# Fused attention and two MoE layers: three of six float32 attention tiles moved to float16 parts with DMA transpositions, and a new list of the front

## The chip, the cores and the metric

The kernel runs on one core of one Trainium2 chip. The metric is the device time of one execution in microseconds; smaller is better. The core has a matmul engine (TensorE, PE in the profile, with its weight loads as PEld), a vector engine (VectorE, DVE), a scalar engine (ScalarE, ACT), GpSimd (POOL) and SyncE (SP), whose queue issues most DMAs.

## The reference

The block-sparse attention (local band of 32 keys and 24 block summaries) feeds a dense layer with a clipped gate, and its output feeds a mixture of experts in which each token goes to one of eight experts.

```python
# attention: q, k, v are (2, 8, 768, 64)
k_sum = k.reshape(B, H, nb, block, D).max(axis=3)      # block = 32
v_sum = v.reshape(B, H, nb, block, D).mean(axis=3)
scores_l = scale * q @ k.T      # kept where |i - j| < 16
scores_s = scale * q @ k_sum.T + log(block)
a = softmax(concat(scores_l_masked, scores_s))
attn = a @ concat(v, v_sum)
...
# dense layer, x = attn as (1536, 512)
h = x @ w_in                                           # (1536, 2048)
g = h * np.clip(h + 3.0, 0.0, 6.0) / 6.0
x2 = g @ w_out                                         # (1536, 512)
...
# experts: one of 8 for each token, by argmax of x2 @ w_gate
h = np.maximum(xe @ w1[e], 0.0)                        # F = 1024
out[mask] = gate_w[mask, None] * (h @ w2[e])
```

## The kernel before

The 1536 tokens are 12 tiles u of 128, six to a batch. Attention goes tile by tile and in two groups g of four heads: scores (`s`), masking and row maximum (`t`, `nm`), exponentials with their row sums (`e`). Then the probabilities must be turned, because the product with V contracts over keys, and there are two forms of this, chosen for each tile by `F32_T`.

In the float32 form (tiles 0 to 5 before) VectorE takes the reciprocal of the row sums (`r`, `rc`), POOL spreads it over a diagonal matrix (`dg`, line 464), and TensorE multiplies the probabilities by the diagonal, which turns and normalises them in one go (`px`, lines 476 and 479, 16 matmuls of a group). ScalarE and VectorE copy the result out of PSUM (`pc`, `pd`, lines 488 and 490), and TensorE multiplies by V in float32 (`pv`, line 500, 16 matmuls of a group). The result comes out already transposed, and is split into a high and a low float16 part by ScalarE (`xa`) and VectorE (`xp`, line 556). The summaries of V for this form lie in `v2f`, which shares its memory with `v2`.

In the float16 form (tiles 6 to 11 before) ScalarE makes the high part of the probabilities (`pa`, line 453), POOL the low part (`pp`, lines 458 and 459), and a DMA on SP's queue transposes both (`px`, line 470). V is split into parts as well (`va`, `vd`). The product is 40 float16 matmuls of a tile (`pv`, line 517); then VectorE normalises (`n`, line 542), ScalarE and POOL split (`xa`, `xp`, lines 551 and 560), and a second DMA transposes x (`xx`, line 577).

The dense layer takes two tiles at a time (index j): `la` is one of eight groups of 24 matmuls of its first product (line 589), `lr`, `lm`, `lg`, `lp` are the gate on ScalarE, VectorE, ScalarE and POOL, `lb` the second product (line 626). Its weights come as 64-bit floats in 32 chunks of 512 KB (`wl`, 16 of w_in and then 16 of w_out) and are turned into float32 by three integer passes on VectorE (`wx`, `wy`, `ww`), scaled and rounded on ScalarE (`wa`, `wb`) and given a low part by POOL (`wp`). `la` with number m needs chunks 2m and 2m+1.

The order of the early work is written out by hand in the string `FRONT`: each name is a step, and each engine executes the instructions of its steps in this order. Loads of K and q (`kl`, `ld`), copies of V rows (`vu`) and transpositions stand in the same list and go to SP's queue in its order. The string `THEN` holds steps with due positions that are sorted in between later steps. Behind the front come the remaining tiles of attention, the dense layer, the routing of tokens, and the experts, whose steps are chosen by branches on the counts of tokens.

Of the kernel before, what the change touches and what calls it, by code (L numbers as in the profile page):

```python
# [83 lines left out]
FRONT = """
    km0.0 km0.1 km0.2 km0.3 km0.4 km0.5 kf0 s0.0 s0.1 t0.0 s1.0 t0.1 kl1.0 vm0.0 nm0.0 nm0.1 e0.0 t1.0 vm0.1 wl3
    nm1.0 e0.1 r0.0 vm0.2 rc0.0 dg0.0 wx0 e1.0 px0.0 r0.1 wy0 rc0.1 vm0.3 ww0 wl4 pc0.0 dg0.1 pd0.0 wa0 r1.0
    vm0.4 wb0 rc1.0 wp0 px0.1 wx1 dg1.0 vm0.5 pc0.1 ld2 pd0.1 wl5 wy1 vm0.6 wl6 km1.0 px1.0 pvs0 ww1 wx2 wa1
    pd1.0 wb1 wy2 wp1 pvd0 pv0.0 wg pvc0 ww2 pc1.0 pv0.1 wx3 wa2 wx4 s1.1 xa0 wy3 wb2 s2.0 kl1.1 t1.1 wp2 xp0
    nm1.1 wy4 e1.1 t2.0 s2.1 wx5 vu1 r1.1 nm2.0 vu2 rc1.1 e2.0 ww3 dg1.1 kl1.2 wx6 wa3 px1.1 ww4 wb3 r2.0 wl7
    wy5 wp3 pv1.0 ld3 pc1.1 pd1.1 wa4 rc2.0 t2.1 pv1.1 wb4 dg2.0 wy6 xa1 vu3 wp4 px2.0 xp1 nm2.1 la0.0 pc2.0  # L90
    pd2.0 e2.1 wx7 ww5 wy7 wl8 r2.1 pv2.0 ww6 lr0.0 rc2.1 wl9 lm0.0 s3.0 dg2.1 wa5 ww7 wa6 t3.0 lg0.0 wb5 lp0.0
    s3.1 km1.1 wb6 nm3.0 wl10 wp5 kl1.3 wx8 la0.1 wa7 e3.0 km1.2 wp6 wy8 ww8 wb7 r3.0 la0.2 wx9 lr0.1 wp7 rc3.0
    wl11 wy9 wa8 lm0.1 dg3.0 wb8 ww9 lg0.1 wp8 km1.3 la0.3 lr0.2 wl12 lm0.2 lp0.1 wa9 lg0.2 wb9 lp0.2 px2.1
    lr0.3 wp9 lm0.3 pc2.1 ld4 pd2.1 wx10 px3.0 lg0.3 t3.1 lp0.3 pv2.1 pc3.0 pd3.0 wy10 nm3.1 xa2 vu4 ww10 s4.0
    e3.1 xp2 pv3.0 t4.0 wl13 s4.1 r3.1 nm4.0 wa10 rc3.1 dg3.1 e4.0 kl1.4 px3.1 wx11 wb10 r4.0 wy11 wp10 pc3.1
    ld5 rc4.0 t4.1 dg4.0 ww11 wl14 pd3.1 wa11 px4.0 wx12 nm4.1 wb11 wy12 e4.1 wp11 km1.4 ww12 pv3.1 vml1.0 pd4.0
    vml1.2 pc4.0 r4.1 s5.0 vu5 rc4.1 xa3 wx13 dg4.1 la0.4 wl15 wx14 wa12 wy13 wb12 wy14 vha0 wp12 ww13 wl16 xp3
    lr0.4 pv4.0 ww14 wa13 lm0.4 wl17 px4.1 t5.0 wb13 lg0.4 wp13 vhd0 wa14 la0.5 ld6 pc4.1 lp0.4 wb14 wx15 vml1.1
    nm5.0 wp14 wy15 e5.0 s5.1 pd4.1 la0.6 ww15 kl1.5 t5.1 lr0.5 vha1 lm0.5 wl18 wx16 wa15 pv4.1 vhd1 lg0.5 wb15
    wy16 lp0.5 la1.0 lr0.6 r5.0 vha2 wp15 lm0.6 rc5.0 lg0.6 ww16 dg5.0 wl19 nm5.1 la1.1 lr1.0 lp0.6 wa16 wx17  # L100
    e5.1 lm1.0 wy17 la1.2 km1.5 lg1.0 ww17 wb16 lp1.0 kf1 lr1.1 wl20 wp16 wa17 lm1.1 s6.0 lr1.2 r5.1 wb17 la1.3
    lg1.1 wx18 wp17 rc5.1 wy18 lp1.1 lm1.2 wx19 lg1.2 lb0.0 dg5.1 ww18 lr1.3 wy19 wl21 lp1.2 wa18 lm1.3 wb18
    ww19 lg1.3 px5.0 vhd2 wp18 wl22 vml1.3 wa19 vml1.4 la0.7 t6.0 pc5.0 lp1.3 wb19 wx20 wp19 pd5.0 wy20 s6.1 xa4
    wx21 lr0.7 nm6.0 lb0.1 xp4 e6.0 wy21 lm0.7 ww20 lg0.7 ww21 pv5.0 wl23 lp0.7 wl24 wa20 la1.4 wa21 wb20 wb21
    wp20 pa6.0 wp21 la1.5 wx22 lr1.4 wy22 pp6.0 lm1.4 wx23 lg1.4 ww22 lb0.2 lp1.4 lr1.5 px6.0 wy23 wl25 lm1.5
    wa22 wx24 wb22 ww23 lg1.5 wp22 la1.6 wl26 wy24 wa23 lp1.5 ww24 wb23 wl27 wp23 wa24 px5.1 lr1.6 wb24 lm1.6
    lb0.3 wp24 pc5.1 ld7 pd5.1 t6.1 lg1.6 lp1.6 nm6.1 pv5.1 e6.1 la1.7 wx25 wy25 xa5 r6 pa6.1 ww25 rc6 wl28
    pp6.1 xp5 wa25 s7.0 lr1.7 la2.0 t7.0 wb25 wp25 lm1.7 wx26 lg1.7 nm7.0 wy26 lp1.7 lb0.4 e7.0 ww26 lr2.0 pa7.0
    lm2.0 vm1.0 la2.1 vha3 wx27 pp7.0 lg2.0 vhd3 wl29 wa26 lp2.0 wb26 wy27 vml1.5 la2.2 lr2.1 ww27 wp26 wl30
    lm2.1 wa27 wx28 lg2.1 wy28 wb27 la2.3 lp2.1 lr2.2 ww28 wl31 init lm2.2 wp27 wa28 wx29 lg2.2 wy29 lb0.5 wb28  # L110
    lp2.2 wx30 lr2.3 ww29 wp28 lm2.3 wa29 wy30 lg2.3 vm1.1 wb29 ww30 la2.4 lp2.3 vha4 wx31 wa30 wp29 vhd4 wb30
"""

THEN = """
    wp30 51.05, wy31 52.5, ww31 52.5, wa31 52.5, wb31 52.5, wp31 52.5, vm1.2 52.85, vm1.3 54.2, vml1.6 55.2,
    vm1.4 55.2, vha5 56.2, vhd5 56.2, vm1.5 56.2, vha6 57.2, vhd6 57.2, vm1.6 57.2, pvs1 57.2, pvd1 57.2,
    pvc1 57.2, lr2.4 58.47, lm2.4 58.47, lg2.4 58.47, lp2.4 58.47, vl1.1 59.75, la2.5 60.47, lr2.5 60.47,
    lm2.5 60.47, lg2.5 60.47, lp2.5 60.47, lb0.6 61, vl1.0 61.37, va1.1 61.75, vd1.1 61.75, la2.6 62.47,
    lr2.6 62.47, lm2.6 62.47, lg2.6 62.47, lp2.6 62.47, lb0.7 63, va1.0 63.37, vd1.0 63.37, xoa0 63.5, xo0 63.5,
    la2.7 64.47, lr2.7 64.47, lm2.7 64.47, lg2.7 64.47, lp2.7 64.47, lb1.0.0 65, xoa1 65.08, xo1 65.08,  # L120
    lb1.0.1 66, px6.1 66.37, vl1.2 66.52, lb1.0.2 67, va1.2 67.04, vd1.2 67.04, lb1.0.3 68, pv6.0 68.37,
    pv6.1 68.37, n6 68.37, xa6 68.37, xp6 68.37, xx6 68.37, lb1.1.0 69, lb1.1.1 70, xoa2 70.96, xo2 70.96,
    lb1.1.2 71, s7.1 71.75, t7.1 71.75, nm7.1 71.75, e7.1 71.75, px7.0 71.75, lb1.1.3 72, xoa3 72.5, xo3 72.5,
    pa7.1 72.75, pp7.1 72.75, px7.1 72.75, lb2.0.0 73, vu7 73.25, lb2.0.1 74, r7 74.75, rc7 74.75, pv7.0 74.75,
    pv7.1 74.75, n7 74.75, xa7 74.75, xp7 74.75, xx7 74.75, lb2.0.2 75, lb2.0.3 76, lb2.1.0 77, lb2.1.1 78,
    lb2.1.2 79, xoa4 79.7, xo4 79.7, lb2.1.3 80, xoa5 80.5, xo5 80.5, la3.0 81, lr3.0 81, lm3.0 81, lg3.0 81,
    lp3.0 81, la3.1 82, lr3.1 82, lm3.1 82, lg3.1 82, lp3.1 82, la3.2 83, lr3.2 83, lm3.2 83, lg3.2 83,
    lp3.2 83, la3.3 84, lr3.3 84, lm3.3 84, lg3.3 84, lp3.3 84, la3.4 85, lr3.4 85, lm3.4 85, lg3.4 85,
    lp3.4 85, la3.5 86, lr3.5 86, lm3.5 86, lg3.5 86, lp3.5 86, la3.6 87, lr3.6 87, lm3.6 87, lg3.6 87,
    lp3.6 87, la3.7 88, lr3.7 88, lm3.7 88, lg3.7 88, lp3.7 88  # L130
"""


# [269 lines left out]

# [844 lines left out]
```

## Time and profile before

| what | value |
|---|---|
| three runs | 542.65, 547.66, 539.81 us; median 542.65 |
| profiled execution, its own time | 537.69 us |
| span of its trace | 535.9 us |
| TensorE busy | 491.1 us of the span |
| mean granted clock of TensorE | 0.97 |

The profile is of one execution. Its span lies inside its own time. Matmuls are pipelined: the duration of one is longer than the distance to the next, so a stream of matmuls is measured from start to start.

### The profile page before, as it was taken

To read this page: it belongs to the slowest core of one execution; us is meant where nothing else is said; L and a number is where in the kernel's file an instruction comes from. 1 tells how busy PE (TensorE), PEld (TensorE's weight loads), DVE (VectorE), ACT (ScalarE), POOL (GpSimd) and SP (SyncE) were. 2 spreads that over 40 slices of the span, in tenths; PEclk is the share of its full clock that TensorE was granted. 3 is DMA by queue.
4 is the path that set the end of the run, shared out by engine and by line. 5 is a ranking of instruction groups with operands and counts; after the bars stand their busy time and mean duration, and the time that the engine had idled before them with its cause. 6 is when DMAs were issued, how large, how long until landed. Compare 5 with 4: busy or idle time off the path is not lost. (4 is left out here: it accounts for less than half of the span.)

```text
span 535.9 us, 11697 instructions
## 1 busy us (share of the span) xinstructions
PE 491.1 (92%) x4528; PEld 333.6 (62%) x4528; DVE 273.6 (51%) x774; ACT 249.5 (47%) x532; POOL 189.2 (35%) x182
## 2 busy tenths in 40 slices
PE   5969888999999999999999999799999989997991
...
PEclk9897998999999999999999999999999989998996
...
GB/s 266 337 123 135 201 133 206 162 103 238 95 242 60 119 129 85 153 53 41 138 70 46 65 60 258 227 254 129 22 161 295 133 251 287 266 306 169 44 9 16
DMA packets 95578, 81.53 MB, mean 152 GB/s; under 512 B 61647, under 2 KB 76239, under 8 KB 95504
## 3 DMA queue, kind: packets, MB, share of 16 engines
...
## 5 line engine op out<-in xcount | busy, mean ns | idle before, releaser
L589 PE MATMUL hps<-xt,wih 128*128 128x256 f16 x768 | 129.1, 273 | 4.9 <-DVE slot L684 3.2
L626 PE MATMUL x2ps<-wo,gt 128*128 128x512 f16 x576 | 129.6, 379 | 0.0
L589 PE MATMUL hps<-xt,wil 128*128 128x256 f16 x384 | 104.8, 273 | 0.0
L626 PEld LDWEIGHTS <-gt 128*128 128x128 f16 x576 | 54.7, 98 | 62.6 <-issue 1.5
L589 PEld LDWEIGHTS <-wih 128*128 128x128 f16 x768 | 73.4, 98 | 18.9 <-DVE rel L600 5.0
L610 POOL TENSOR_TENSOR gt<-rel,gt 128x512 f16<-128x512 f32 x48 | 58.0, 1212 | 35.8 <-ACT gt L608 35.5
L830 PEld LDWEIGHTS <-w1t 128*128 128x128 f16 x1152 | 62.0, 98 | 8.6 <-issue 1.8
L848 PE MATMUL yp<-w2t,hh 128*128 128x512 f16 x240 | 57.6, 387 | 3.8 <-ACT hh L834 3.4
L444 ACT ACTIVATE s<-s,nm 128x184 f32<-128x184 f32 x88 | 38.2, 436 | 34.5 <-DVE nm L439 34.5
L835 DVE SCALAR_TENSOR_TENSOR hh<-hp,hh 128x512 f16<-128x512 f32 (+1 forms) x30 | 18.4, 618 | 58.2 <-ACT hh L834 58.1
L600 DVE SCALAR_TENSOR_TENSOR rel<-rel,hps 128x512 f32<-128x512 f32 x48 | 32.8, 682 | 25.7 <-ACT rel L596 25.5
L848 PEld LDWEIGHTS <-hh 128*128 128x128 f16 x264 | 24.8, 99 | 30.4 <-ACT hh L834 3.8
L830 PE MATMUL hp<-xb,w1t 128*128 128x128 f16 x672 | 40.9, 219 | 0.0
L589 PEld LDWEIGHTS <-wil 128*128 128x128 f16 x384 | 37.6, 98 | 4.8 <-issue 0.4
L596 ACT ACTIVATE rel<-hps,brelu 128x512 f32<-128x512 f32 x48 | 32.6, 679 | 14.4 <-PE hps L589 11.3
L608 ACT ACTIVATE gt<-rel 128x512 f16<-128x512 f32 x48 | 30.0, 624 | 17.3 <-DVE rel L600 16.8
L834 ACT ACTIVATE hh<-hp 128x512 f16<-128x512 f32 (+1 forms) x30 | 16.0, 539 | 41.7 <-PE hp L830 41.7
L415 PE MATMUL ps<-kx,qraw 64*128 64x184 f32 x192 | 24.0, 368 | 10.0 <-DVE nm L431 5.1
...
L431 DVE CUSTOM_DVE_ANT_0 s<-ps,cf 128x184 f32<-128x184 f32 x88 | 25.6, 343 | 7.8 <-PE ps L415 6.1
L415 PEld LDWEIGHTS ps<-kx,qraw 64*128 64x128 f32 x192 | 16.6, 203 | 16.5 <-DVE nm L431 6.2
L458 POOL TENSOR_TENSOR pb<-s,pb 128x512 f16<-128x512 f32 x12 | 13.9, 1157 | 36.2 <-ACT pb L453 27.1
...
## 6 DMA issues: line engine op xcount, KB each, us to landing
...
```

The costliest lines, as they stand in the source:

```text
L415: nc.tensor.matmul(out=ps[i % 2][:, o:o + KC], lhsT=qraw[u][p, h // 2, :], rhs=kx[p, t, h // 2, :], start=True, stop=True)
L431: nc.vector.tensor_tensor_reduce(out=s[:, i, :], in0=ps[i % 2][:, o:o + KC], in1=mask, scale=1.0 / C_S, scalar=-3e38, op0=ALU.add, op1=ALU ...
L444: nc.scalar.activation(s[:, i, :], s[:, i, :], AF.Exp, bias=nm[:, i:i + 1], accum_out=sums[u][:, 4 * g + i:4 * g + i + 1])
L589: nc.tensor.matmul(out=hps[:, c, :], lhsT=w[:, kk, f:f + 128], rhs=xt[j][:, a * KD + kk, :], start=(i == 0), stop=(i == 3 * KD - 1))
L596: nc.scalar.activation(rels[j, m], hs[j, m], AF.Relu, scale=S_G / (S_X * S_WI) ** 2, bias=brelu)
L600: nc.vector.scalar_tensor_tensor(out=r, in0=r, scalar=6.0 * S_G / (S_X * S_WI), in1=hs.pop((j, m)), op0=ALU.min, op1=ALU.mult)
L608: nc.scalar.activation(gh, rels[j, m], AF.Copy)
L610: nc.gpsimd.tensor_tensor(out=gl, in0=rels.pop((j, m)), in1=gh, op=ALU.subtract)
L626: nc.tensor.matmul(out=o, lhsT=gts[j][:, a, f, i * 128:(i + 1) * 128], rhs=w[:, f, :], start=(f == 0 and n == 0), stop=(f == KF - 1 and n ...
L830: sp["mm"] = nc.tensor.matmul(out=hp[:, c, :], lhsT=w1t[:, a, kk, f:f + 128], rhs=x[:, b * KD + kk, 0:n], start=(i == 0), stop=(i == 3 * K ...
L835: ve.scalar_tensor_tensor(out=hh[:, 1, m * 4:m * 4 + 4, :], in0=hp, scalar=0.0, in1=hi, op0=ALU.max, op1=ALU.subtract)
L848: nc.tensor.matmul(out=yp, lhsT=hh[:, a, f, :], rhs=w2t[:, b, f, :], start=(f == 0 and i == 0), stop=(f == FK - 1 and i == 2))
```

## The change

`F32_T` is cut to tiles 0 to 2, so tiles 3 to 5 take the float16 form. Because batch 0 now has tiles of both forms, the summaries of V are made in both: `pvs0`, `pvd0`, `pvc0` in float16 parts, and new steps `pvf0`, `pvg0` in float32. `v2f` no longer shares memory with `v2`; it lies in the float32 view of the low half of w_out's tile (`wof[1]`, columns 1536 to 2559). `FRONT` is written anew: 573 steps instead of 548. It leaves out the steps `dg`, `pc`, `pd` of tiles 3 to 5 and holds `pa`, `pp`, `n`, `xx` for them, `va` and `vd` for V of tiles 3 to 6, and the steps of tiles 6 and 7 and of batch 1's V summaries that stood in `THEN`. The steps of `la1.7` and `la2.4` have left the list for `THEN`, which has 120 steps instead of 141.

```diff
-F32_T = (0, 1, 2, 3, 4, 5)
+F32_T = (0, 1, 2)
...
-    nm1.0 e0.1 r0.0 vm0.2 rc0.0 dg0.0 wx0 e1.0 px0.0 r0.1 wy0 rc0.1 vm0.3 ww0 wl4 pc0.0 dg0.1 pd0.0 wa0 r1.0
-    vm0.4 wb0 rc1.0 wp0 px0.1 wx1 dg1.0 vm0.5 pc0.1 ld2 pd0.1 wl5 wy1 vm0.6 wl6 km1.0 px1.0 pvs0 ww1 wx2 wa1
-    pd1.0 wb1 wy2 wp1 pvd0 pv0.0 wg pvc0 ww2 pc1.0 pv0.1 wx3 wa2 wx4 s1.1 xa0 wy3 wb2 s2.0 kl1.1 t1.1 wp2 xp0
-    nm1.1 wy4 e1.1 t2.0 s2.1 wx5 vu1 r1.1 nm2.0 vu2 rc1.1 e2.0 ww3 dg1.1 kl1.2 wx6 wa3 px1.1 ww4 wb3 r2.0 wl7
-    wy5 wp3 pv1.0 ld3 pc1.1 pd1.1 wa4 rc2.0 t2.1 pv1.1 wb4 dg2.0 wy6 xa1 vu3 wp4 px2.0 xp1 nm2.1 la0.0 pc2.0
-    pd2.0 e2.1 wx7 ww5 wy7 wl8 r2.1 pv2.0 ww6 lr0.0 rc2.1 wl9 lm0.0 s3.0 dg2.1 wa5 ww7 wa6 t3.0 lg0.0 wb5 lp0.0
...
+    nm1.0 e0.1 r0.0 vm0.2 rc0.0 dg0.0 wx0 e1.0 px0.0 r0.1 wy0 rc0.1 vm0.3 ww0 va0.4 wl4 dg0.1 pd0.0 pc0.0 r1.0
+    wa0 vm0.4 va0.5 vd0.4 wb0 px0.1 vd0.5 va0.3 wp0 rc1.0 km1.0 vm0.5 vd0.3 pc0.1 ld2 dg1.0 wl5 pd0.1 s1.1 wl6
+    wx1 vm0.6 kl1.1 t1.1 pvf0 pvs0 pvg0 px1.0 wy1 pvd0 ww1 pvc0 pv0.0 pd1.0 wa1 nm1.1 wx2 e1.1 pv0.1 wx3 wy2
+    s2.0 wy3 wb1 ww2 xa0 wp1 t2.0 pc1.0 wa2 s2.1 xp0 wb2 wx4 kl1.2 wp2 t2.1 wy4 wx5 vu1 nm2.0 vu2 wy5 e2.0 r1.1
+    wx6 nm2.1 wy6 e2.1 pv1.0 ww3 rc1.1 ww4 dg1.1 r2.0 wl7 wa3 wa4 px1.1 ww5 wb3 rc2.0 ww6 wb4 dg2.0 r2.1 wl8 ld3
+    pc1.1 wl9 wp3 px2.0 pd1.1 wa5 wx7 wa6 rc2.1 wp4 wb5 wy7 pv1.1 wb6 pd2.0 ww7 pc2.0 wp5 wl10 km1.2 vu3 s3.0
+    xa1 wp6 km1.1 wa7 xp1 wb7 dg2.1 pv2.0 t3.0 wp7 wx8 px2.1 nm3.0 wy8 e3.0 s3.1 ld4 pd2.1 ww8 kl1.3 la0.0 t3.1
+    wl11 pa3.0 wg nm3.1 pc2.1 pp3.0 e3.1 pv2.1 px3.0 lr0.0 la0.1 wx9 vu4 pa3.1 r3 lm0.0 wa8 pp3.1 wy9 lg0.0 rc3
+    ww9 wb8 la0.2 km1.3 lr0.1 lp0.0 px3.1 wl12 lm0.1 xa2 ld5 wp8 lg0.1 xp2 wa9 la0.3 wx10 lp0.1 lr0.2 wb9 wy10
+    lm0.2 wp9 wx11 lg0.2 ww10 s4.0 lr0.3 lp0.2 wy11 pv3.0 wl13 wa10 lm0.3 wx12 wb10 lg0.3 ww11 wp10 pv3.1 wl14
+    wy12 wa11 n3 lp0.3 wb11 ww12 xa3 wp11 t4.0 wl15 wa12 s4.1 wx13 xp3 wb12 nm4.0 la0.4 wp12 kl1.4 wy13 e4.0 xx3
+    wx14 ww13 wy14 wl16 wa13 wx15 lr0.4 ww14 wb13 lm0.4 wl17 wp13 la0.5 wy15 lg0.4 t4.1 wa14 lp0.4 pa4.0 ww15
+    wb14 pp4.0 nm4.1 wl18 s5.0 lr0.5 wa15 wp14 px4.0 wx16 la1.0 wb15 lm0.5 e4.1 vml1.1 wp15 wy16 vml1.0 wx17
...
-    v2f = [x.rearrange("p a c -> p (a c)").bitcast(F32) for x in v2]
+    v2f = [wof[1][:, 1536 + i * DM:1536 + (i + 1) * DM] for i in range(2)]
...
     def vm_out(b, part):
-        if b == 1 or not F32_T:
+        if part == 2:
+            nc.scalar.activation(v2f[0], pvm[b], AF.Copy)
+        else:
             split(v2[0][:, 0], v2[0][:, 1], pvm[b], S_V if b == 0 else 1.0, part)
-        elif part == 0:
-            nc.scalar.activation(v2f[0], pvm[b], AF.Copy)
-
-    def vm_copy(b):
-        w = v2f if b == 0 and F32_T else v2
+
+    def vm_copy(w):
         for p0 in (32, 96):
             nc.sync.dma_start(out=w[1][p0:p0 + 32], in_=w[0][p0:p0 + 32])
...
-                 pvd=lambda b: vm_out(b, 1), pvc=vm_copy, wl=first, wx=lambda i: w_word(i, 0), wy=lambda i: w_word(i, 1),
+                 pvd=lambda b: vm_out(b, 1), pvc=lambda b: vm_copy(v2),
+                 pvf=lambda b: vm_out(b, 2), pvg=lambda b: vm_copy(v2f), wl=first, wx=lambda i: w_word(i, 0), wy=lambda i: w_word(i, 1),
```

## Rows read from the trace of the kernel before

**Rows 1.** The page's parts 1 and 2: TensorE's share, its slices, its granted clock.

```profile
PE 491.1 (92%) x4528; PEld 333.6 (62%) x4528; DVE 273.6 (51%) x774; ACT 249.5 (47%) x532; POOL 189.2 (35%) x182
...
PE   5969888999999999999999999799999989997991
...
PEclk9897998999999999999999999999999989998996
```

**Rows 2.** Stretches: busy us (instructions) of PE, PEld, DVE, ACT, POOL; clock, DMA.

```profile
60.00:90.00 30.00, 25.09 (x233) 18.87 (x231) 25.16 (x75) 21.26 (x53) 16.30 (x15) 0.95 0.57 178
90.00:120.00 30.00, 30.00 (x255) 22.60 (x253) 24.77 (x58) 21.40 (x52) 16.93 (x16) 1.00 0.41 126
120.00:150.00 30.00, 30.00 (x243) 21.39 (x240) 19.67 (x46) 21.78 (x47) 18.90 (x19) 1.00 0.60 166
150.00:180.00 30.00, 29.73 (x212) 19.85 (x210) 22.70 (x49) 22.88 (x50) 17.49 (x19) 1.00 0.44 140
```

**Rows 3.** Timeline of TensorE near 131 and 136 us: start, length, instruction, count.

```profile
131.36 1.06 PE L476 MATMUL ph<-dg,s 128*128 128x128 f32 x8
132.35 0.65 PE L479 MATMUL ph<-dg,s 128*64 128x128 f32 x8
132.93 1.25 PE L626 MATMUL x2ps<-wo,gt 128*128 128x512 f16 x5
...
135.62 0.44 PE L500 MATMUL po<-pf,wo 128*64 128x128 f32 x4
...
137.09 0.39 PE L589 MATMUL hps<-xt,wih 128*128 128x256 f16 x2
137.32 0.27 PE L589 MATMUL hps<-xt,wil 128*128 128x256 f16 x1
137.43 0.38 PE L589 MATMUL hps<-xt,wih 128*128 128x256 f16 x2
```

**Rows 4.** Timeline of TensorE before 90 us; in brackets the wait and its releaser.

```profile
38.13 0.89 PE L415 MATMUL ps<-kx,qraw 64*128 64x184 f32 x8 [3.88 <-DVE nm L431]
...
48.84 0.39 PE L589 MATMUL hps<-xt,wih 128*128 128x256 f16 x2
...
86.63 1.93 PE L476 MATMUL ph<-dg,s 128*128 128x128 f32 x8
```

**Rows 5.** Timeline of TensorE: first of 40 matmuls of tile 6, and what follows.

```profile
191.96 0.25 PE L517 MATMUL po<-vt,pt 128*128 128x64 f16 x3
...
193.13 3.19 PE L626 MATMUL x2ps<-wo,gt 128*128 128x512 f16 x14
```

**Rows 6.** Groups of ScalarE, 0 to 180 us: busy us, mean ns, idle before.

```profile
L488 ACT ACTIVATE pf<-ph 128x512 f32<-128x512 f32 x12 | 7.2, 597 | 5.8 <-PE ph L476 4.6 <-PE po L500 1.1
...
L453 ACT ACTIVATE pb<-s 128x736 f16<-128x736 f32 x4 | 3.2, 804 | 0.0
L216 ACT ACTIVATE vt<-vraw 128x512 f16<-128x512 f32 x3 | 1.9, 620 | 1.1 <-DMA vraw<-in_v_dram 1.1
```

**Rows 7.** Groups of VectorE, 0 to 180 us, in the same columns.

```profile
L490 DVE COPY pf<-ph 120x256 f32<-120x256 f32 x12 | 5.0, 419 | 7.4 <-PE ph L479 4.8 <-PE po L500 2.6
...
L218 DVE SCALAR_TENSOR_TENSOR vt<-vraw,vt 128x512 f16<-128x512 f32 x3 | 2.0, 683 | 2.4 <-ACT vt L216 2.4
```

**Rows 8.** Line 533, the sums for the diagonals: ns min/median/max, first and last start.

```profile
L533 DVE TENSOR_SCALAR rg<-sums x12: 158/170/1152, 19.5 to 105.7; 128x4 f32<-128x4 f32 x12
```

**Rows 9.** Groups of POOL, 0 to 240 us, in the columns of rows 6.

```profile
L464 POOL TENSOR_TENSOR dg<-ch,rg 128x512 f32<-128x512 f16 x12 | 13.2, 1103 | 32.8 <-DVE rg L537 32.8
L458 POOL TENSOR_TENSOR pb<-s,pb 128x512 f16<-128x512 f32 x7 | 8.1, 1159 | 19.8 <-ACT pb L453 15.5 <-issue 4.2
...
L459 POOL TENSOR_TENSOR pb<-s,pb 128x224 f16<-128x224 f32 x7 | 4.3, 612 | 0.0
```

**Rows 10.** DMA issues of the run: count, median us from issue to landing.

```profile
pt<-pb SPq DMA_TRANSPOSE x12, 4.4
...
xt<-xc SPq DMA_TRANSPOSE x6, 3.2
```

More of the change, by code (lines that the diff above doesn't have):

```diff
@@ L84 @@
 FRONT = """
-    km0.0 km0.1 km0.2 km0.3 km0.4 km0.5 kf0 s0.0 s0.1 t0.0 s1.0 t0.1 kl1.0 vm0.0 nm0.0 nm0.1 e0.0 t1.0 vm0.1 wl3
-    nm1.0 e0.1 r0.0 vm0.2 rc0.0 dg0.0 wx0 e1.0 px0.0 r0.1 wy0 rc0.1 vm0.3 ww0 wl4 pc0.0 dg0.1 pd0.0 wa0 r1.0
-    vm0.4 wb0 rc1.0 wp0 px0.1 wx1 dg1.0 vm0.5 pc0.1 ld2 pd0.1 wl5 wy1 vm0.6 wl6 km1.0 px1.0 pvs0 ww1 wx2 wa1
-    pd1.0 wb1 wy2 wp1 pvd0 pv0.0 wg pvc0 ww2 pc1.0 pv0.1 wx3 wa2 wx4 s1.1 xa0 wy3 wb2 s2.0 kl1.1 t1.1 wp2 xp0
-    nm1.1 wy4 e1.1 t2.0 s2.1 wx5 vu1 r1.1 nm2.0 vu2 rc1.1 e2.0 ww3 dg1.1 kl1.2 wx6 wa3 px1.1 ww4 wb3 r2.0 wl7
@@ L90 @@
-    wy5 wp3 pv1.0 ld3 pc1.1 pd1.1 wa4 rc2.0 t2.1 pv1.1 wb4 dg2.0 wy6 xa1 vu3 wp4 px2.0 xp1 nm2.1 la0.0 pc2.0
-    pd2.0 e2.1 wx7 ww5 wy7 wl8 r2.1 pv2.0 ww6 lr0.0 rc2.1 wl9 lm0.0 s3.0 dg2.1 wa5 ww7 wa6 t3.0 lg0.0 wb5 lp0.0
-    s3.1 km1.1 wb6 nm3.0 wl10 wp5 kl1.3 wx8 la0.1 wa7 e3.0 km1.2 wp6 wy8 ww8 wb7 r3.0 la0.2 wx9 lr0.1 wp7 rc3.0
-    wl11 wy9 wa8 lm0.1 dg3.0 wb8 ww9 lg0.1 wp8 km1.3 la0.3 lr0.2 wl12 lm0.2 lp0.1 wa9 lg0.2 wb9 lp0.2 px2.1
-    lr0.3 wp9 lm0.3 pc2.1 ld4 pd2.1 wx10 px3.0 lg0.3 t3.1 lp0.3 pv2.1 pc3.0 pd3.0 wy10 nm3.1 xa2 vu4 ww10 s4.0
@@ L95 @@
[L95 to L109, printed above, removed]
@@ L110 @@
-    lm2.1 wa27 wx28 lg2.1 wy28 wb27 la2.3 lp2.1 lr2.2 ww28 wl31 init lm2.2 wp27 wa28 wx29 lg2.2 wy29 lb0.5 wb28
-    lp2.2 wx30 lr2.3 ww29 wp28 lm2.3 wa29 wy30 lg2.3 vm1.1 wb29 ww30 la2.4 lp2.3 vha4 wx31 wa30 wp29 vhd4 wb30
+    km0.0 km0.1 km0.2 km0.3 km0.4 km0.5 kf0 s0.0 s0.1 t0.0 kl1.0 s1.0 t0.1 vm0.0 nm0.0 nm0.1 e0.0 t1.0 vm0.1 wl3
+    nm1.0 e0.1 r0.0 vm0.2 rc0.0 dg0.0 wx0 e1.0 px0.0 r0.1 wy0 rc0.1 vm0.3 ww0 va0.4 wl4 dg0.1 pd0.0 pc0.0 r1.0
+    wa0 vm0.4 va0.5 vd0.4 wb0 px0.1 vd0.5 va0.3 wp0 rc1.0 km1.0 vm0.5 vd0.3 pc0.1 ld2 dg1.0 wl5 pd0.1 s1.1 wl6
@@ new lines @@
+    wb14 pp4.0 nm4.1 wl18 s5.0 lr0.5 wa15 wp14 px4.0 wx16 la1.0 wb15 lm0.5 e4.1 vml1.1 wp15 wy16 vml1.0 wx17
+    ww16 lg0.5 lr1.0 la0.6 wy17 lp0.5 wl19 r4 wa16 lm1.0 pa4.1 ww17 lg1.0 pp4.1 t5.0 la0.7 wb16 lr0.6 rc4 wl20
+    nm5.0 lp1.0 px4.1 wa17 lm0.6 e5.0 km1.4 ld6 la1.1 wp16 wx18 wy18 lg0.6 ww18 wb17 lp0.6 wl21 pv4.0 wa18 wp17
+    s5.1 lr1.1 lr0.7 kl1.5 t5.1 lb0.0 wb18 pa5.0 lm1.1 wp18 lm0.7 lg1.1 pp5.0 wx19 lg0.7 nm5.1 la1.2 lp1.1 px5.0
+    wy19 e5.1 wx20 lp0.7 ww19 pv4.1 wy20 lr1.2 r5 wl22 wx21 va0.6 lm1.2 pa5.1 la1.3 vd0.6 lg1.2 pp5.1 wy21 vu5
```

40 lines of the change are left out of this document (24 added, 16 removed).

## The prediction

> **What bounds the kernel now.** I read the page's busy shares and its forty slices first, for the engine that never rests, then the table of stretches, for where it does rest, and then the timeline of TensorE, for what one group of the work in question takes. TensorE is the bound: it is busy for 92% of the span, and after the first sixth of the slices its row shows nines almost to the end, at the full granted clock [rows 1]. It is short of work before 90 us: 25.09 of 30 us from 60 to 90, then 30.00, 30.00 and 29.73 [rows 2]. A busy digit alone proves little, but in the timeline the matmuls of layer one follow each other there at an even pitch, three in 0.34 us, 24 (one group, a step la) in 2.6 to 2.7 [rows 3]. So TensorE work taken out behind 90 us is worth its full length, as long as the other engines keep up. In front of that it is worth something only where TensorE was not waiting anyhow: it waited 3.88 us for the vector engine's softmax before 38.13, and behind such waits the clock falls to its lower level, 1.2 GHz. Eight turning matmuls span 1.93 us at 86.63 and 1.06 us at 131.36 [rows 3, 4]. Tiles 3 to 5, which the change touches, run from about 66 to 137 us, most of it in or near the saturated part.
>
> **What leaves TensorE.** One group of four heads in float32 is turned in two runs of eight matmuls, which begin at 131.36; the next work begins at 132.93: 1.57 us. Its product with V begins at 135.62 and the next work at 137.09: 1.47 us, both at full clock [rows 3]. Together 3.04 us, six groups: 18.2 us.
>
> **What comes in.** The product in float16 parts is 40 matmuls to a tile. The trace shows it for tiles 6 and later: it begins at 191.96 and the next work at 193.13, 1.17 us for the 40 [rows 5]. The duration of one would mislead, since they overlap; the starts count. Three tiles: 3.5 us. The transpositions by DMA take no TensorE time. So TensorE's stream is shorter by 18.2 - 3.5 = 14.7 us; what it does otherwise is the same, in another order.
>
> **What the other engines get.** ScalarE loses six copies of 0.597 us and gains six p_hi of 0.804, four V parts (tiles 3 to 6) and one more copy of the V means, 0.620 each [rows 6]: -3.6 + 4.8 + 3.1 = +4.3 us. x_hi stays one pass. VectorE loses six copies of 0.419 and twelve small ops (0.170 the median); it gains five low parts at 0.683 (four of V, one of the means) and six small ops; the norm takes the place of the low x, which goes to POOL [rows 7, 8]: -2.5 - 2.0 + 3.4 + 1.0, about 0. POOL loses six diagonals of 1.103 and gains six p_lo of 1.159 + 0.612 and three low x of the first of these sizes: -6.6 + 10.6 + 3.5 = +7.5 us [rows 9]; it has room, 16 to 19 of 30 us busy [rows 2]. SP gets six transpositions of p and three of x, which land 4.4 and 3.2 us after issue [rows 10], and two small copies of the means (pvg0). None of this is on TensorE's path unless it comes late.
>
> **Whether it comes late.** px4.0 stands four layer-one groups ahead of pv4.0 in the new list, and the other pairs of tiles 4 and 5 no less than three groups of layer one or two: over 7 us, against a landing of 4.4. Tile 3 is tighter. From s3.1 to pv3.1 TensorE has four layer-one groups, pv2.1, a score group (0.89) and pv3.0: some 13 us. The chain softmax, exp, p_hi 0.80, p_lo 1.77, issue and landing is some 10 and has other steps between: I put nothing on it, up to 3 us. Tile 3's x is tightest: norm, x_hi, POOL's 1.16, landing 3.2, with ScalarE's and POOL's weight steps between, some 9 us, against two score groups and two layer-one groups, 7 us, ahead of la1.0. I put 2 us on it. Behind px3.1 in SP's queue waits the load of q for tile 5, behind px4.1 that for tile 6; their score groups come several layer-one groups later, which hides it; without that cover it would be a landing, some 4 us, once. The new place of v2f is in the part of wo's low half that chunks 22 to 25 fill, so wp22 to wp25 must wait for tile 2's product; they stand over two hundred steps behind it: nothing.
>
> **The new order at the beginning.** Before, layer one begins at 48.84 [rows 4]. In the new list pv2.0, px2.1 and two score groups have moved ahead of la0.0: 1.47 + 1.57 + 2 x 0.89 = 4.8 us, which is work and no loss. The loss: the copies vu1 now stand behind kl1.2 on SP, which must wait until s2.1 has read its K tile, and pv1.0 and px1.1 wait for vu1 on TensorE. The old trace has TensorE idle near here anyhow (the 3.88 us), so this is from 0 to +4 us; I take +2, and layer one begins near 55.5.
>
> **How full the shorter stretch is.** From 60 to 150 us ScalarE was busy 21.26 + 21.40 + 21.78 = 64.4 us and VectorE 25.16 + 24.77 + 19.67 = 69.6 [rows 2]. If these 90 us shrink to 75.3, ScalarE has to carry 64.4 + 4.3 in them, and five passes more that the list pulls forward (eight of tile 7, of V and of layer two come in, three of layer one go out), 2.5 us at an estimate from [rows 6]. Three more of the 32 weight chunks stand ahead of la0.0 and are done earlier, two passes each: -3.7. That is 67.5 of 75.3, 90%. VectorE: 69.6, 2 us pulled forward, less four chunks of three passes (near 0.683 each), 8.2: 63.4, 84%. The fullest 30 us of the old trace are 22.88 for ScalarE (76%) and 25.16 for VectorE (84%), so ScalarE would be fuller than it has yet been, though nothing asked it to be. In the other direction, the waits of tiles 3 to 5 on diagonals, on copies out of PSUM and on the low x disappear: TensorE stood still for 4.9 us from 60 to 90, and lost 0.9 to the clock in the run at 86.63. So the waits change by between -6 us (all of these gone, nothing new) and +14 us (ScalarE held to 76%: 67.5/0.76 = 89 us instead of 75). I take +2: 2 for the beginning, 2 for tile 3's x, 4 for a full ScalarE, less 6 for the waits that go.
>
> **The sum.** -14.7 + 2 = -12.7, call it -13 us. The profiled execution takes 537.69 us by its own time (span 535.9), which gives 524.7. It was faster than the median of the three runs, 542.65, by 0.9%; on the median the same sum is 529.65. I predict 529.5. A measurement of this kernel can tell some 2% from no change, 10.9 us.
>
> **A rule against it.** POOL's longer work can hold up VectorE: the small sums for the diagonals take from 0.158 to 1.152 us [rows 8]. The Trainium skill has a rule for such stretching (SBUF — State Buffer, Who interferes with whom): VectorE and GpSimd share one pair of ports under an exclusive lock, and whoever comes second is blocked for the whole instruction. By that rule up to all of POOL's additional 7.5 us could be added to VectorE's 63.4, 71 of 75, and it would lead to the first rival below. The trace agrees as far as the small operations go; how much of it a longer list would show, no row tells.
>
> **The rivals.** (a) ScalarE and VectorE set the pace of the shorter stretch: TensorE, done early with each piece, waits for the next relu or weight chunk, and the clock falls behind the waits. For it: the 90% and 84%, in engines that hand work to each other in a written order. Against: from 60 to 90 VectorE did run at 84%. It costs 4 to 10 us more than the forecast: -9 to -3, 534 to 540. (b) The old waits go and nothing new comes: -17 to -20, 523 to 526. For it: they belong to the form that leaves; against: the full ScalarE. (c) The gain is taken back at the end, where the expert stage waits for weights and TensorE is no longer saturated: 0 to -3, 540 to 543. Against: that stage starts by results which then come earlier. (d) Slower: the transpositions land exposed. One late p_lo holds every later load and transposition in SP's queue, and each group's product waits on TensorE for its landing. Nine transpositions have 6 x 4.4 + 3 x 3.2 = 36 us of landing; if all of it shows, +21 us, 564. It turns into a loss from 14.7/9 = 1.6 us shown for each, and passes 2% from 2.8. Against it: the distances in the list above.
>
> **How the numbers follow.** The forecast (-10 to -16) 0.55; (a) 0.22; (b) 0.10; (c) 0.05; (d) 0.08. The range 521 to 540 holds the forecast on either base (521.7 is -16 on the profiled time), (b) and (a). Faster by over 2% (under 531.8): 0.50 of the forecast and (b), 0.60. Within 2%: 0.05 of it, (a) and (c), 0.32. Slower: (d), 0.08.
>
> **What would show it.** In the changed profile: the turning matmuls and the float32 products at half their count; six more transpositions of p and three of x before 140 us; the first layer-one matmul near 55 us; TensorE without long idle time from about 80 us; the end of the front some 13 us earlier. Wrong would be ScalarE at over nine tenths while TensorE waits for relu or weight steps (a), or TensorE waiting for transpositions (d). A beginning in which TensorE idles much longer than 2 us more, with a fallen clock behind it, would prove me wrong as well.

## The result, and the profile after

The changed kernel takes 530.1 us (median of 5 executions, 524.85 to 534.84), the kernel before 544.47 beside it (median of 5): a ratio of 0.9722, with a 95% interval from 0.967 to 0.9774. Measured twice more, each time beside the kernel before, it gave 0.9867 [0.9806, 0.9929] and 0.9768 [0.9708, 0.9828] (`same` and `same_b` below). Ratios and their intervals leave out every execution that is more than 1.5% above the fastest of the same kernel. So the gain is 1.3 to 2.8%, 7 to 15 us, and two measurements of one kernel can lie 8 us apart. The profiled execution of the changed kernel (534.33 us) was one of its longer ones; where stretches are compared I use `same_b`, the same kernel in an execution of 524.15.

The page of the changed kernel, in the parts of [rows 1]: TensorE has 72 matmuls fewer on record and is busy 11.9 us less; its slices are no fuller at the beginning, and the eleventh and twelfth (133 to 160 us) are eights, where [rows 1] has nines.

```profile
PE 479.2 (90%) x4456; PEld 325.1 (61%) x4456; DVE 283.8 (53%) x767; ACT 251.5 (47%) x537; POOL 197.2 (37%) x191
...
PE   5877978999889999999999999799988989799991
...
PEclk9986978999999999999999999999999999899996
```

The stretches of `same_b` (columns as in [rows 2]). Against [rows 2] VectorE (the third pair) is the fullest side engine, up to 27.41 of 30 us, and TensorE no longer reaches 30 before 150 us.

```profile
60.00:90.00 30.00, 24.16 (x233) 19.89 (x231) 26.70 (x60) 25.39 (x57) 20.86 (x20) 0.94 0.84 211
90.00:120.00 30.00, 28.75 (x279) 21.50 (x277) 25.17 (x54) 24.40 (x53) 24.43 (x23) 1.00 0.98 206
120.00:150.00 30.00, 25.99 (x183) 16.63 (x181) 27.41 (x59) 21.98 (x55) 17.27 (x19) 1.00 0.76 222
150.00:180.00 30.00, 29.62 (x219) 20.01 (x218) 14.91 (x41) 14.91 (x33) 16.26 (x15) 1.00 0.38 92
```

TensorE's timeline in the changed kernel at the beginning: scores at the low clock, its stop for the copies vu1, the next turning, still at the low clock, and the first layer-one matmul, which stood at 48.84 [rows 4].

```profile
36.36 1.60 PE L413 MATMUL ps<-kx,qraw 64*128 64x184 f32 x8 [1.85 <-DVE nm L429]
...
41.80 2.15 PE L498 MATMUL po<-pf,wo 56*64 56x128 f32 x12 [3.22 <-DMA wo<-wo]
44.19 2.08 PE L474 MATMUL ph<-dg,wo 128*128 128x128 f32 x8 [0.24 <-POOL dg L462]
...
53.05 1.54 PE L498 MATMUL po<-pf,wo 128*64 128x128 f32 x16 [0.77 <-DVE xt L554]
...
57.02 0.39 PE L587 MATMUL hps<-xt,wih 128*128 128x256 f16 x2
```

Behind the stop of 3.22 us, twelve product matmuls take 2.15 us; sixteen take 1.54 at 53.05, when the clock is back. The clock had fallen before that stop: the eight score matmuls at 36.36, behind a stop of 1.85 us, take 1.60 us, where eight take 0.89 at full clock [rows 4]. In the same profile, the stops inside tiles 3 and 4: for a transposed part, for VectorE's softmax, and for tile 3's transposed x.

```profile
71.59 0.26 PE L515 MATMUL po<-vt,pt 128*128 128x64 f16 x3 [0.83 <-DMA pt<-pb]
...
75.23 1.60 PE L413 MATMUL ps<-kx,qraw 64*128 64x184 f32 x8 [2.88 <-DVE nm L429]
...
86.95 0.38 PE L587 MATMUL hps<-xt,wih 128*128 128x256 f16 x2 [1.47 <-DMA xt<-xc]
```

How the granted clock answers (the third column from the end), in three stretches around those stops. From 70 to 78 us VectorE is busy for all of the 8 us while TensorE has work for 4.28.

```profile
36.00:50.00 14.00, 10.18 (x58) 7.53 (x60) 11.43 (x34) 10.25 (x29) 7.83 (x8) 0.51 0.64 190
70.00:78.00 8.00, 4.28 (x56) 3.29 (x55) 8.00 (x20) 6.37 (x16) 6.38 (x6) 0.73 0.87 258
86.00:92.00 6.00, 5.05 (x32) 3.85 (x33) 4.00 (x8) 4.20 (x13) 4.54 (x6) 0.72 1.08 250
```

The transpositions in `same` (columns of [rows 10]): six more of p and three more of x, with medians of 3.7 and 3.3 us from issue to landing (4.4 and 3.2 before). Single ones of x took up to 11.4, and in `same_b` the median of x was 8.4; in neither did TensorE wait for one, so the distances in the list cover that too.

```profile
pt<-pb SPq DMA_TRANSPOSE x18, 3.7
...
xt<-xc SPq DMA_TRANSPOSE x9, 3.3
```

What the part up to the end of attention gained is read from one row: when the last score group of the kernel starts (the last number), in the kernel before and in `same_b`.

```profile
L415 PE MATMUL ps<-kx,qraw x192: 316/316/672, 12.2 to 296.4; 64*128 64x184 f32 x192
```

```profile
L413 PE MATMUL ps<-kx,qraw x192: 315/317/673, 11.9 to 288.0; 64*128 64x184 f32 x192
```

That is 8.4 us earlier (4.2 in the first profile, 7.8 in `same`). From there to the end of the span all 14 profiles of this study take between 234 and 242 us, the kernel before 239.5, `same` 241.3, `same_b` 234.4, for nearly the same work. So two profiles of one kernel differ there by up to 7 us; the row of the last scores itself differs by 4 us between the three profiles of the changed kernel.

### The profile page after: what moved, and what is told of

Read it like the earlier page. It is cut to its first block, busy times and chain, and to the rows that moved or that the text cites. A ratio compares the mean times of both kernels' runs of the same rounds, so it can differ in the third digit from the quotient of the medians.

```text
span 532.5 us, 11590 instructions
## 1 busy us (share of the span) xinstructions
PE 479.2 (90%) x4456; PEld 325.1 (61%) x4456; DVE 283.8 (53%) x767; ACT 251.5 (47%) x537; POOL 197.2 (37%) x191
## 5 line engine op out<-in xcount | busy, mean ns | idle before, releaser
L587 PE MATMUL hps<-xt,wih 128*128 128x256 f16 x768 | 131.5, 277 | 7.2 <-DVE slot L682 3.4
L587 PE MATMUL hps<-xt,wil 128*128 128x256 f16 x384 | 106.2, 277 | 0.0
L587 PEld LDWEIGHTS <-wih 128*128 128x128 f16 x768 | 74.9, 99 | 23.5 <-issue 5.6
L833 DVE SCALAR_TENSOR_TENSOR hh<-hp,hh 128x512 f16<-128x512 f32 (+1 forms) x30 | 18.4, 618 | 56.4 <-ACT hh L832 48.3
L606 ACT ACTIVATE gt<-rel 128x512 f16<-128x512 f32 x48 | 29.9, 625 | 17.8 <-DVE rel L598 17.6
L456 POOL TENSOR_TENSOR pb<-s,pb 128x512 f16<-128x512 f32 x18 | 20.9, 1160 | 35.9 <-issue 24.8
```

What stands on the lines that cost most here:

```text
L456: nc.gpsimd.tensor_tensor(out=p[:, :, 256:384], in0=s[:, :, 0:c1], in1=p[:, :, 0:c1], op=ALU.subtract)
L587: nc.tensor.matmul(out=hps[:, c, :], lhsT=w[:, kk, f:f + 128], rhs=xt[j][:, a * KD + kk, :], start=(i == 0), stop=(i == 3 * KD - 1))
L606: nc.scalar.activation(gh, rels[j, m], AF.Copy)
```

## The experiments

Twelve runs in three sets; each set ran on one chip beside the kernel before, and each ratio is against that. "Last scores" is the row just shown, from one profiled execution. The profiled executions of `pe_back`, `dve_more` and `vsum_late` lie 7.5, 2.6 and 8.1 us above the median of their run, and their last scores are late for this reason too.

| run | edit | ratio [95%] | last scores |
|---|---|---|---|
| same, same_b | none | 0.9867 [0.9806, 0.9929], 0.9768 [0.9708, 0.9828] | 288.6, 288.0 |
| pe_back | 17.6 us of TensorE work added | 1.0076 [1.0039, 1.0114] | 307.5 |
| pe_less | 14 us of TensorE work removed | 0.9853 [0.9795, 0.9911] | 286.0 |
| vu1_early | copies vu1 earlier | 0.9809 [0.9753, 0.9866] | 288.0 |
| old_list | new form, old list | 1.0126 [1.0057, 1.0194] | 307.9 |
| dve_more | 8.3 us of VectorE work added | 0.9907 [0.9862, 0.9951] | 297.1 |
| act_more | 7.5 us of ScalarE work added | 0.9815 [0.9766, 0.9864] | 288.8 |
| vsum_late | V summary of batch 1 later | 0.9851 [0.978, 0.9922] | 308.1 |
| vu1_dg | vu1 and dg1.1 earlier | 0.9808 [0.9748, 0.9867] | 288.7 |
| t4_early | t4.0 earlier | 0.9805 [0.975, 0.986] | 293.1 |
| mended | both of these | 0.9813 [0.9747, 0.9879] | 290.5 |

**Is it the stream of TensorE?** First the unaltered kernel, then the stream made longer and shorter.

> The changed kernel once more, unaltered, to have its time beside the other runs of this chip and a second trace. Its ratio to the kernel before should be near the first one, 0.972, that is some 15 us less. If the trace of the first look, whose span is only 3.4 us shorter than that of before, is typical, the ratio is near 0.99; if it was a disturbed execution, the new span is near 523 us and the front ends earlier than in the first trace.

> The changed kernel with TensorE's work put back and nothing else: ahead of each group's float16 product of tiles 3 to 5 stand 12 float32 matmuls of 128x128 by 128x128 on constants, whose results the product overwrites. 12 of about 0.245 us (four take 0.98 in the trace of before), six groups: 17.6 us. Theory (TensorE's stream is what the change shortens, and the rest has room): the time rises by 16 to 18 us over the changed kernel, to about the kernel before or slightly above. Rival (ScalarE and VectorE set the pace of the new front): the matmuls fall into time in which TensorE waits, the waits behind 120 us in the trace shrink, and the rise is 5 to 10 us.

```diff
+        if u in (3, 4, 5):
+            for _ in range(12):
+                nc.tensor.matmul(out=o[:, 256 * g:256 * g + 128], lhsT=cf[:, 0:128], rhs=cf[:, 0:128], start=True, stop=True)
```

> The changed kernel with TensorE's work cut further and nothing else: in layer one the product with the low part of the weights is left out for the first four tiles (j = 0 and 1), 8 of 24 matmuls in 16 groups, each 0.109 us: 14 us less for TensorE, 13 of it in the front. Less of the computation is done, the output is less exact. Theory (TensorE is the bound): 11 to 14 us less than the changed kernel. Rival (ScalarE and VectorE set the pace): TensorE only waits longer, 0 to 5 us less, and its idle share in the front rises by what was cut.

```diff
-                for w, a in ((wih, 0), (wih, 1), (wil, 0)):
+                parts = ((wih, 0), (wih, 1)) if j < 2 else ((wih, 0), (wih, 1), (wil, 0))
+                for w, a in parts:
...
```

With the work put back, the ratio rises by 0.0209, 11 us of the 17.6, which lies between the theory's 16 to 18 and the rival's 5 to 10, and the gain is gone: it hangs on TensorE's shorter stream. No run has the old form in the new list; `pe_back`, which has the new list and a stream as long as before, comes nearest to it and is no faster than the kernel before. But 14 us less than the changed kernel gives nothing that can be measured (0.9853 beside 0.9867), and 2.0 to 2.6 us at the last scores, which is within their spread. The waits of `pe_less` from 60 to 120 us (total, times, longest) say where the rest went; `same_b` has 4.8 us on the first of these lines and 1.3 on the second, and none on the other two:

```profile
PE ps L413 <- DVE nm L429: 5.3, 2, 4.0
PE hps L588 <- DVE rel L599: 3.5, 3, 2.2
PE hps L588 <- DMA xt<-xc: 2.0, 1, 2.0
PE po L515 <- DMA pt<-pb: 2.0, 1, 2.0
```

So the change has brought the front to the point where more TensorE work costs about two thirds of its length and less gives next to nothing. The other engines set the pace from here on.

**Is it the form, or the list?**

> The float16 form of tiles 3 to 5 is put into the list of the kernel before: where that list has the diagonal of a group, the group's high and low parts are made, the transposition stays where the turning was, the float32 copies drop out, and the V summary of batch 1 goes behind tile 5. Theory (the new list is needed, since a group's parts and its transposition, 0.8 + 1.8 + 1.4 + 4.4 us from the rows, have to be issued long before the product): TensorE is busy as little as in the changed kernel, but waits for the transposed parts 2 to 4 us at each of the six groups, so that the time is 538 to 552. Rival (the form alone brings the gain): 528 to 535 with waits for transposed parts under 1 us in all but one group.

```diff
-... dg3.0 ... pc3.0 pd3.0 ... dg4.0 ... vml1.0 ... vha0 ...   (FRONT of the kernel before)
+... pa3.0 pp3.0 ...           ... pa4.0 pp4.0 ...  (batch 1's vml, vha, vhd, vm behind xx5)
```

The form in the old order is slower than the kernel before by 1.3%, some 7 us, and than the changed kernel by some 14 to 22. TensorE's two worst stops, and the stretches they lie in:

```profile
78.86 0.34 PE L519 MATMUL po<-vt,pt 128*128 128x64 f16 x3 [5.58 <-DMA pt<-pb]
```

```profile
136.75 0.34 PE L519 MATMUL po<-vt,pt 128*128 128x64 f16 x3 [7.24 <-DMA pt<-pb]
```

```profile
60.00:90.00 30.00, 21.45 (x203) 17.12 (x202) 21.84 (x66) 21.01 (x51) 18.11 (x19) 0.72 0.83 186
...
120.00:150.00 30.00, 18.62 (x132) 12.50 (x131) 16.25 (x47) 14.67 (x36) 13.69 (x14) 0.84 0.79 166
```

The theory foresaw 2 to 4 us at each of six groups; it is 12.8 us at two of them and 5.5 more at transposed x. The new list is what hides the transpositions: in the first profile above they cost tiles 3 to 5 0.83 us of waiting for p and 1.47 for x. In the old list this was rival (d) of the prediction.

**Which engine holds the front now?**

> The first integer pass of twelve of the weight blocks (12 to 23, whose passes lie at about 70 to 115 us) is made twice: 12 passes of 0.69 us, 8 us of VectorE more and nothing else. Theory (behind 60 us VectorE now sets the pace, 28 of 30 us at 120:150, so that TensorE's 14 us less in one run came to some 3 us): 5 to 8 us slower than the unaltered one. Rival 1 (ScalarE sets it): 0 to 3 us slower. Rival 2 (TensorE's stream sets it): at most 2 us slower.

```diff
-            nc.vector.tensor_scalar(out=words[i], in0=st[:, :, 1], ...)
+            for _ in range(2 if 12 <= i < 24 else 1):
+                nc.vector.tensor_scalar(out=words[i], in0=st[:, :, 1], ...)
```

> The high part of the same twelve weight blocks is written twice: 12 instructions of 0.62 us, 7.5 us of ScalarE more and nothing else. Theory (VectorE sets the pace): 0 to 3 us slower than the unaltered one. Rival 1 (ScalarE, 25.4 and 24.3 of 30 us at 60:120, sets it): 5 to 8 us slower. Rival 2 (TensorE's stream sets it): at most 2 us slower.

```diff
-        nc.scalar.activation(hi, st, AF.Copy)
+        for _ in range(2 if 12 <= i < 24 else 1):
+            nc.scalar.activation(hi, st, AF.Copy)
```

ScalarE's 7.5 us vanish: 0.9815 is among the unaltered values, and the last scores stand at 288.8. VectorE's 8.3 us show: the ratio is 0.9907, 5 us over `act_more` in the same set (the two intervals touch at their ends), and the last scores stand at 297.1, 4.9 to 9.1 us later than in the three profiles of the unaltered kernel. Against the three values of the unaltered kernel (0.9722, 0.9768, 0.9867), none of them from this set, the timed cost lies between 2 and 10 us, so its size is not settled, only which engine. In `dve_more` TensorE stops for the weights themselves:

```profile
81.70 0.38 PE L588 MATMUL hps<-xt,wih 128*128 128x256 f16 x2 [2.14 <-DVE y L251]
...
90.03 0.38 PE L588 MATMUL hps<-xt,wih 128*128 128x256 f16 x2 [2.00 <-DVE y L251]
```

> The loads, splits and sums of batch 1's V summary, which the new list has moved to 120 to 157 us, go to the end of the front list, behind px6.0 (about 140 to 175 us, where VectorE is half idle). Theory (VectorE is full at 120:150 and TensorE waits there 2.8 us for the summary's splits and 2.2 us for layer-two weights): these waits go, 3 to 6 us faster than the unaltered one. Rival (the integer passes pace that stretch anyway, or the summary's loads wait for their two buffers and stop TensorE at the end): from 0 to 4 us slower.

```diff
-... vml1.1 ... n5 vha0 vha1 vhd0 ... vm1.0 ... (spread from px4.0 on)
+... px6.0 ... the same steps, in their order, evenly to the end of FRONT
```

No gain is seen: 0.9851, a ratio of the three shorter executions (528.99, 534.47 and 534.93 us); the other three take 544.62 to 547.88, and the profiled one (547.88) is the longest. There ScalarE waits for the summary's rows of V, which have two buffers (total, times, longest), and TensorE behind it, 5.0 us for the split and 4.8 for a layer-two weight that ScalarE had queued behind:

```profile
ACT vh L216 <- DMA vraw<-in_v_dram: 8.3, 3, 4.4
```

What it does in its shorter executions was not profiled, so this run says that the theory's 3 to 6 us were not seen, and why in one execution.

**Can the stops be taken out of the list?**

> The changed kernel with one step moved: the copies vu1 of V rows go ahead of kl1.2 in SP's queue, right behind pvg0. In the trace of the changed kernel TensorE waits 3.22 us for this copy from 38.6 to 41.8, and the turning groups behind it run at the lower clock (2.08 us for eight matmuls instead of 1.1). Theory (the wait stands on the path of the beginning): layer one begins 3 to 6 us earlier than at 57 us, and the time falls by 2 to 5 us. Rival (the front is paced by VectorE and ScalarE, which go on meanwhile): layer one begins earlier but the time falls by less than 1.5 us. It can also be that the next thing, the diagonal of tile 1's second half, is late at the same point: then neither moves by more than 1 us.

```diff
-... pvf0 pvs0 pvg0 px1.0 ... wx5 vu1 nm2.0 ...
+... pvf0 pvs0 pvg0 vu1 px1.0 ... wx5 nm2.0 ...
```

> The copies vu1 stand right behind pvg0 as in vu1_early, and the softmax steps r1.1, rc1.1 and the diagonal dg1.1 stand 8 to 13 places earlier in the list, where exps e1.1 has been done since 34.3 us. Theory (TensorE's stop at 39.4 to 43 us belongs to whichever of the two chains, the copies or the diagonal, is late, and the granted clock stays at 1.2 GHz from 37 to 47 us because of it): with both early the stop of 3.2 to 3.7 us goes and the low clock ends sooner; first layer-one matmul at 50 to 53 us instead of 55.2, time 3 to 6 us under the unaltered kernel. Rival (a third chain, the exponentials of tile 2 or the float32 copies of a group, is as late): first layer-one at 54 to 55, within 2 us of the unaltered kernel.

```diff
-s2.0 wy3 wb1 ww2 xa0 wp1 t2.0 pc1.0 wa2 ... e2.0 r1.1 wx6 ... ww3 rc1.1 ww4 dg1.1
+s2.0 wy3 t2.0 r1.1 wb1 ww2 xa0 wp1 rc1.1 pc1.0 dg1.1 wa2 ... e2.0 wx6 ... ww3 ww4
```

The stop of 3.2 us for vu1 went, and TensorE stood as long at the next instruction, first for the diagonal (`vu1_early`), then, with that early too, for the following group (`vu1_dg`), where the profile names ScalarE's weight copy:

```profile
43.12 2.07 PE L474 MATMUL ph<-dg,wo 128*128 128x128 f32 x8 [3.74 <-POOL dg L462]
```

```profile
46.03 2.08 PE L473 MATMUL ph<-dg,s 128*128 128x128 f32 x8 [4.86 <-ACT wih L274]
```

First layer-one matmul: 55.2 and 56.4, where the unaltered kernel has 55.2 and 55.5. In `vu1_dg` the group's own diagonal comes just as late: GpSimd makes it from 44.67 to 45.98, after sums that VectorE takes of exponentials for which ScalarE had waited until 40.86, behind VectorE's nm. So the third chain of the rival is there, and it too leads back to VectorE.

> The step t4.0 (VectorE reads the scores of tile 4's first group out of PSUM) stands right behind wy11, some ten VectorE passes earlier; nothing else moves. Theory (TensorE's longest stop, 3.9 us before the scores s4.1 at 73.4 us, is no lack of VectorE throughput but the place of one step in its order: the scores were done at 68.2 and were read at 72.2 behind seven weight passes): the stop shrinks to under 1 us and the low clock at 74 to 77 us with it, 2 to 5 us under the unaltered kernel. Rival (VectorE is full from 61 to 78 us, so the weights that were pushed back make TensorE wait as long at the next layer-one group): within 1.5 us of it.

```diff
-lp0.2 wy11 pv3.0 wl13 ... ww12 xa3 wp11 t4.0 wl15 wa12 s4.1
+lp0.2 wy11 t4.0 pv3.0 wl13 ... ww12 xa3 wp11 wl15 wa12 s4.1
```

In the unaltered kernel the scores s4.0 are made at 67.33; VectorE reads them at 72.18, behind passes over weights; only then is their PSUM room free for s4.1. VectorE and TensorE of `same`:

```profile
68.00 0.69 DVE L246 SCALAR_TENSOR_TENSOR bits<-stg,bits 128x512 int32<-128x512 int32 x1
...
71.58 0.68 DVE L250 SCALAR_TENSOR_TENSOR y<-stg,bits 128x512 int32<-128x512 int32 x1
72.18 0.34 DVE L429 CUSTOM_DVE_ANT_0 s<-ps,cf 128x184 f32<-128x184 f32 x1
```

```profile
67.33 0.89 PE L413 MATMUL ps<-kx,qraw 64*128 64x184 f32 x8
...
73.39 0.90 PE L413 MATMUL ps<-kx,qraw 64*128 64x184 f32 x8 [3.89 <-DVE nm L429]
```

In `t4_early` this stop is 0.30 us, and two others have taken its place, at layer one for the weights (y) that t4.0 was put ahead of:

```profile
71.09 0.90 PE L413 MATMUL ps<-kx,qraw 64*128 64x184 f32 x8 [0.30 <-DVE nm L429]
72.97 0.38 PE L587 MATMUL hps<-xt,wih 128*128 128x256 f16 x2 [0.98 <-DVE y L250]
...
80.14 0.59 PE L587 MATMUL hps<-xt,wih 128*128 128x256 f16 x2 [4.39 <-DVE y L250]
```

3.89 us have become 0.30 + 0.98 + 4.39. The time is not shorter (0.9805).

> Both of the list's edits together: vu1, r1.1, rc1.1, dg1.1 and t4.0 earlier. Theory (the gain that did not come is held by single places of the new list): the sum of the two, 5 to 11 us under the unaltered kernel, 520 to 526. Rival (VectorE and ScalarE set the pace of the front): not over 3 us under it.

> The changed kernel unaltered, beside the other three on the same chip: 528 to 534 us, 0.98 to 0.99 of the kernel before.

`mended` at 0.9813 beside `same_b` at 0.9768: no version beat the changed kernel. The first and the third set ran on one chip; there the executions of the unaltered kernel (ten of twelve, without the longest of each set) have a mean of 529.2 us; `vu1_early`, `vu1_dg`, `t4_early` and `mended` have 528.7, 528.8, 529.3 and 529.1. The 3 us by which `vu1_early` seemed ahead of `same` were spread between executions: its last scores stand at 288.0, as in `same_b`.

## Why the prediction was right, and which of its terms were not

The time, 529.5 foretold and 530.1 measured, agrees, and -13 us lies between the 7 and 15 that three measurements give. That the two numbers lie 0.6 us apart is luck: measured again, the same kernel gave -7 us, which rival (a) had for itself. The terms agree less well than their sum.

- **The stream, -14.7 us.** It holds. TensorE's busy time is 491.1 before, 475.9 in `same_b`, 478.9 in `same` and 479.2 in the first profile, where the clock was at its lower level for longer. The turning matmuls and float32 products stand at half their count (48 of 96 on each of the two turning lines, 96 of 192 for the products), and `pe_back` shows that the gain hangs on this.
- **The beginning, +2.** Right in size: layer one begins at 57.02, 55.2 and 55.5 for a foretold 55.5, and there is a stop of 3.2 us for vu1. But the wait for vu1 is not what costs the time: with the copies early, layer one begins at 55.2 all the same (`vu1_early`). Nor does TensorE idle longer than before in the first 60 us (12.7 us in `same_b`, 13.8 before); its clock is lower, 0.83 from 30 to 60 us for 0.89.
- **Tile 3's x, +2.** 1.47 us in the first profile, none in `same_b`, where the layer-one group behind it waits 1.1 us for ScalarE instead.
- **The six waits of tiles 3 to 5 that go, -6.** They went, and their room was taken: TensorE idles 24.2 us of the first 180 in `same_b`, 18.9 before (180 less the sums of busy time over the six stretches of 30 us, 155.83 and 161.06). The prediction had the waits at +2 in sum; the last scores, 8.4 us earlier instead of 13 (4.2 in the first profile), say +6 or more.
- **A full ScalarE, +4.** The wrong engine, and this is the step that failed. ScalarE was forecast at 90% of the 75.3 us and VectorE at 84%. In the 75.3 us from 60 on, `same_b` has ScalarE at 60.0 (80%) and VectorE at 65.9 (88%). ScalarE has room for 7.5 us more (`act_more`), and VectorE has none to spare at the stops: rival (a), with VectorE in the chief part. Two things were missed in VectorE's sum, the weights and the lengthening of its instructions. The rows of VectorE from 60 to 150 us, before and in `same_b` (busy, mean ns):

```profile
L244 DVE TENSOR_SCALAR bits<-stg 128x512 int32<-128x512 int32 x19 | 13.1, 687 | 0.7 <-ACT y L272 0.4
...
L218 DVE SCALAR_TENSOR_TENSOR vh<-vraw,vh 128x512 f16<-128x512 f32 x4 | 3.6, 903 | 0.8 <-ACT vh L216 0.8
...
L439 DVE TENSOR_SCALAR nm<-nm 128x4 f32<-128x4 f32 x8 | 2.7, 337 | 0.0
```

```profile
L243 DVE TENSOR_SCALAR bits<-stg 128x512 int32<-128x512 int32 x22 | 15.0, 687 | 3.0 <-DMA stg<-in_moe_w_out_dram 2.7 <-DMA stg<-in_moe_w_in_dram 0.2
...
L217 DVE SCALAR_TENSOR_TENSOR vh<-vraw,vh 128x512 f16<-128x512 f32 x5 | 6.3, 1271 | 0.0
L437 DVE TENSOR_SCALAR nm<-nm 128x4 f32<-128x4 f32 x7 | 5.3, 758 | 0.0
```

The weights: the sum took four blocks out of the stretch because they stand ahead of la0.0 in the list. But la0.0 itself came later, and by 60 us ten blocks had been begun in both kernels. Behind 150 us four were left before and none in `same_b`, where the last one begins at 145.5 instead of 161.5. So the stretch has eleven passes more instead of twelve fewer (22, 23 and 23 of the three kinds for 19 each), 7.2 us.

The lengthening: the softmax's nm (one fewer) goes from 337 to 758 ns, and a low part of V from 903 to 1271. The timelines of `same_b` show when. VectorE, and then GpSimd beside it:

```profile
39.11 0.16 DVE L437 TENSOR_SCALAR nm<-nm 128x4 f32<-128x4 f32 x1
...
140.72 3.40 DVE L217 SCALAR_TENSOR_TENSOR vh<-vraw,vh 128x512 f16<-128x512 f32 x1
...
152.84 1.12 DVE L437 TENSOR_SCALAR nm<-nm 128x4 f32<-128x4 f32 x1
```

```profile
140.19 1.15 POOL L279 TENSOR_TENSOR wo<-y,wo 128x512 f16<-128x512 f32 x1
141.31 1.15 POOL L608 TENSOR_TENSOR gt<-rel,gt 128x512 f16<-128x512 f32 x1
142.42 1.14 POOL L279 TENSOR_TENSOR wo<-y,wo 128x512 f16<-128x512 f32 x1
...
152.32 1.61 POOL L608 TENSOR_TENSOR gt<-rel,gt 128x512 f16<-128x512 f32 x1
```

All eight nm between 60 and 155 us are lengthened (0.43 to 1.12 us), and each ends 0.02 to 0.04 us after a GpSimd instruction that ran beside it; the three at 32.37, 39.11 and 40.23, with none beside them, take 0.16. The low part of V at 140.72 lasts over three GpSimd instructions and ends 0.56 us after the third, while the integer passes take 0.67 to 0.70 beside GpSimd as well. In `vsum_late`, which makes these low parts later, they take 691 ns in the mean (1337 in `same_b`, whole run). An estimate from these rows, taking each lengthened nm, sum and low part less its length beside an idle GpSimd, is 7.8 us from 60 to 150 in `same_b` and 3.1 before. The rule that the prediction named (the Trainium skill, SBUF — State Buffer, Who interferes with whom) speaks of this: VectorE and GpSimd lock a shared pair of ports against each other, which concerns VectorE's instructions in a two-port mode or with two inputs in SBUF. The trace agrees as far as these ends show it. So VectorE's 9.7 us more in these 90 us (69.6 to 79.3) are 7.2 of weights and some 4.7 of waiting for GpSimd, and the rest goes the other way. No run took GpSimd's work away, so what the lengthening costs the kernel's time is not shown.

- **The rivals.** (a) is true in its mechanism but took 4 to 5 us of the front in `same_b` (9 in the first profile), not the whole gain. (b) did not happen: in every list that was run another wait took the place of the one removed. (c) is not seen: the part behind the last scores takes as long as before within its own spread. (d) is what the form does in the old list.

Why a sum with a wrong term came out: the front gave 4 to 8 us in place of 13, and the remainder of any single comparison lies in the spread of the part behind it. What stays open is the exact size of the gain between 7 and 15 us, and what VectorE's waiting for GpSimd costs in time.
